# Token-major keys of the mixing stage by a crossbar transpose instead of TensorE, with C and two of the four mixing steps one group later

## Chip, cores, metric

One core of one Trainium2 chip. The metric is the device time of one launch in microseconds (us). Executions of one kernel on a chip mostly agree within 0.3%.

## The reference

Grouped attention (8 batches, 16 query heads, 4 key heads, 384 tokens, head size 64), then a token mixer on its output `x` (8 x 384 x 1024):

```python
wq = x @ w_q                      # d_hyper = 64
wk = x @ w_k
W_tok = einsum('bsd,btd->bst', wq, wk) / 8
mixed = einsum('bst,btd->bsd', W_tok, x)
out = maximum(mixed, 0) @ w_out
```

The kernel reorders the mixing: first `C = wk^T x` (64 x 1024), then `mixed = wq C`. So it needs wk twice turned: the projection makes `qk` with features on the partitions, and C needs wk with tokens on the partitions ("token-major keys").

## The kernel before

Tiles that matter: the projection, the turned keys, C, and the mixing steps (two matmuls each, one relu per matmul on VectorE).

```python
def proj_task(s):                       # 8 matmuls -> pqk, then qk and q2 (VectorE)
    ...
def wk_task(s):                         # token-major keys, TensorE
    ptw = psX.tile([P, C, P], BF16, name="ptw", tag="ps")
    for c in range(C):
        nc.tensor.transpose(out=ptw[:, c, :], in_=s.qk[:, c * P:(c + 1) * P], identity=ident)
    s.wk = m_p.tile([P, C, Dh], BF16, name="wk", tag="wk")
    nc.vector.tensor_copy(out=s.wk, in_=ptw[:, :, Dh:])
def c_task(s):                          # 6 matmuls pc <- wk, xnat; scaled copy to Csb
    ...
def mix_banks(s, i):                    # one mixing step
    for h in range(2):
        pm = psX.tile([P, S], F32, name="pmb", tag="ps")
        nc.tensor.matmul(out=pm, lhsT=s.Csb[r, i*P:(i+1)*P], rhs=..., start=True, stop=True)
        nc.vector.tensor_relu(out=m, in_=pm)
# ... cut ...
elif b < B - 1:                         # batches 2 to 6; g is the batch's first group after it
    at(g + 4, lambda b=b: proj_task(batches[b]), 1.3)
    todo.setdefault(g + 5, []).insert(0, (lambda b=b: wk_task(batches[b]), 0.17))
    todo.setdefault(g + 6, []).insert(0, (lambda b=b: c_task(batches[b]), 0.75))
    gm = (7, 8, 9, 10)                  # groups at whose end a mixing step stands
```

A group is two score tiles (four `sc` matmuls), their exponentials on ScalarE, and then the group's list: AV products (`av`), the tasks above, and single matmuls of the output projection (`po`) as filler. The order is fixed when the program is built. `psX` has four PSUM buffers, shared by everything except the scores. From batch 2 on all input loads, crossbar transposes (`kT`, `qT`, `xT`) and nearly all output writes go through one queue, that of SyncE, in program order.

## Time and profile before

| | before |
|---|---|
| time, median of 4 | 221.97 us (221.65 to 222.37) |
| TensorE, VectorE, ScalarE busy | 94%, 63%, 66% |
| DMA engines | full to 138 us, then 10 to 70% |
| projection of batch 2, 3, 4, 5, 6, 7 starts at | 77.98, 98.92, 122.87, 146.82, 170.55, 188.19 us |

The last row: from one projection to the next is one batch (nine groups; fewer to batch 7), about 24 us for batches 3 to 5 and 20.9 for batch 2. It comes from the timeline of TensorE, the pqk lines.

### The profile page before, as it was taken

How to read it: one execution, taken by the hardware profiler on the slowest of the kernel's cores; microseconds unless marked ns; L12 is line 12 of the kernel's file. 1: busy time of each engine (PE TensorE's matmuls, PEld its weight loads, DVE VectorE, ACT ScalarE, POOL GpSimd, SP SyncE). 2: the span in 40 equal slices, each digit the busy share in tenths (PEclk: the TensorE clock that was granted, in tenths of full speed). 3: DMA queues.
4: the chain of work that ended last, by engine and by line, in shares of the span. 5: the costliest groups of instructions: out<-in, count | busy, mean ns of one | idle time of the engine just before them, and what ended most of it. 6: DMA issues, size and time to landing. Idle time of an engine off the chain costs nothing.

```text
span 220.2 us, 5371 instructions
## 1 busy us (share of the span) xinstructions
PE 208.0 (94%) x2182; PEld 103.9 (47%) x2182; DVE 139.2 (63%) x367; ACT 145.2 (66%) x156; POOL 47.6 (22%) x107
## 2 busy tenths in 40 slices
PE   1899999999999999999999999999999999999991
PEld 0356766554354545454444545445445444443440
DVE  1358868655866466865686568756677579855530
ACT  3799999837799989867767776777777772001100
POOL 1489403525103420350035003400000000000000
PEclk9999999999999999999999999999999999999998
DMA  7999999999959999999999999763531251233243
GB/s 169 308 293 293 234 231 290 202 234 300 219 177 228 270 211 221 236 276 210 296 294 215 226 324 313 210 181 71 172 98 73 98 106 65 95 135 151 98 184 114
DMA packets 75598, 44.71 MB, mean 203 GB/s; under 512 B 45488, under 2 KB 72624, under 8 KB 75568
## 3 DMA queue, kind: packets, MB, share of 16 engines
q1 hardware_dynamic: 72128, 41.69, 75.9%
q0 software_dynamic: 2112, 2.10, 5.6%
q10 hardware_dynamic: 1328, 0.52, 0.9%
q8 instruction: 19, 0.31, 0.6%
q14 instruction: 11, 0.09, 0.1%
HBM read 23.59 MB, written 12.58 MB: 164 GB/s over the span
## 4 chain that ended last, share of the span: by engine, by line
PE 85%; DVE 5%; ACT 5%; DMA 2%; issue 1%
PE po L341 37%; PE sc L189 17%; PE av L207 16%; ACT pT L195 5%; PE pqk L239 4%; PE pmb L317 3%; PE pc L283 2%; DVE xnat L215 2%; DMA qraw<-in_q_dram 2%; PE ptq L176 2%; PE ptx L224 1%; DVE msb L323 1%; PE ptw L274 1%; DVE rcp_all L214 1%; DVE osb L354 1%
## 5 line engine op out<-in xcount | busy, mean ns | idle before, releaser
L195 ACT ACTIVATE pT<-sc 128x1024 bf16<-128x1024 f32 x144 | 139.1, 1026 | 34.4 <-PE sc L189 34.2
L341 PE MATMUL po<-wout_sb,msb 128*128 128x512 bf16 x384 | 101.9, 379 | 0.2 <-DVE osb L354 0.2
L207 PEld LDWEIGHTS <-pT 128*128 128x128 bf16 x1152 | 44.9, 98 | 18.2 <-issue 8.9
L207 PE MATMUL av<-vbf,pT 128*128 128x65 bf16 x1152 | 51.4, 194 | 0.2 <-DVE msb L323 0.2
L189 PE MATMUL sc<-qT,kT 64*128 64x512 bf16 x288 | 49.5, 393 | 1.5 <-DVE qT L131 0.5
L341 PEld LDWEIGHTS <-msb 128*128 128x128 bf16 x384 | 33.1, 97 | 37.1 <-issue 12.3
L215 DVE TENSOR_TENSOR xnat<-av,rcp_all 128x256 bf16<-128x256 f32 x96 | 40.8, 425 | 3.3
L354 DVE COPY osb<-po 128x512 f32<-128x512 f32 x46 | 31.6, 688 | 16.5 <-PE po L341 16.4
L131 POOL CAST qbf<-qraw 128x512 bf16<-128x512 f32 x46 | 26.9, 622 | 25.5 <-DMA qraw<-in_q_dram 22.5
L323 DVE TENSOR_SCALAR msb<-pmb 128x384 bf16<-128x384 f32 x53 | 27.0, 551 | 8.1 <-PE pmb L317 8.1
L214 DVE RECIPROCAL rcp_all<-av 128x4 f32<-128x4 f32 x96 | 17.1, 178 | 19.6 <-PE av L207 19.1
L189 PEld LDWEIGHTS <-kT 64*128 64x128 bf16 x288 | 12.7, 94 | 20.9 <-issue 17.7
L131 POOL CAST kbf<-kraw 128x384 bf16<-128x384 f32 x15 | 7.7, 510 | 66.6 <-DMA kraw<-in_k_dram 66.6
L306 ACT ACTIVATE msb<-pm 128x768 bf16<-128x768 f32 x2 | 1.6, 811 | 19.9 <-PE pm L300 19.9
L239 PE MATMUL pqk<-xT,wqk_sb 128*128 128x384 bf16 x56 | 10.3, 327 | 0.0
L317 PE MATMUL pmb<-qk,Csb 64*128 64x384 bf16 x32 | 9.3, 331 | 0.2 <-DVE Csb L292 0.2
L317 PEld LDWEIGHTS <-Csb 64*128 64x128 bf16 x56 | 3.3, 93 | 11.4 <-issue 6.2
L245 DVE CAST qk<-pqk 128x384 bf16<-128x384 f32 x7 | 3.9, 557 | 7.5 <-PE pqk L239 7.5
L292 DVE TENSOR_SCALAR Csb<-pc 128x512 bf16<-128x512 f32 (+1 forms) x9 | 5.6, 631 | 4.8 <-PE pc L283 4.8
L317 PE MATMUL pmb<-q,Csb 64*128 64x384 bf16 x24 | 8.0, 332 | 0.4 <-DVE xnat L215 0.2
L129 ACT COPY osb<-po 128x256 f32<-128x256 f32 x2 | 0.7, 373 | 11.2 <-DVE osb L131 11.2
L131 POOL CAST vbf<-vraw 128x384 bf16<-128x384 f32 x16 | 8.0, 506 | 0.0
(54 smaller groups left out, 81.3 us busy)
## 6 DMA issues: line engine op xcount, KB each, us to landing
out_dram<-osb SPq DMA_DIRECT2D x23, 512.0 KB, 3.1
qraw<-in_q_dram SPq DMA_DIRECT2D x30, 384.0 KB, 5.0
kraw<-in_k_dram SPq DMA_DIRECT2D x16, 192.0 KB, 4.6
vraw<-in_v_dram SPq DMA_DIRECT2D x16, 192.0 KB, 4.8
wout_sb<-in_moe_w_out_dram POOLq DMA_DIRECT2D x4, 512.0 KB, 12.2
qraw<-in_q_dram SPq DMA_DIRECT2D x1, 512.0 KB, 5.3
qraw<-in_q_dram ACTq DMA_DIRECT2D x1, 256.0 KB, 4.0
wraw<-in_moe_w_q_dram SPq DMA_DIRECT2D x1, 256.0 KB, 6.4
```

Of the source, the lines that this page charges most:

```text
L131: eng.tensor_copy(out=out, in_=in_)
L189: nc.tensor.matmul(out=ps[:, h, :], lhsT=s.kT[r, d, c, :], rhs=s.qT[d][r, j, :, :].rearrange("p g n -> p (g n)"), start=True, stop=True)
L195: nc.scalar.activation(out=s.pT[d, j][:, c, :, :], in_=ps, func=AF.Exp, scale=attn_scale)
L207: nc.tensor.matmul(out=av[:, i, :], lhsT=pT[:, c, h, i * P:(i + 1) * P], rhs=s.vbf[:, g, c, :], start=(c == 0), stop=(c == C - 1))
L214: nc.vector.reciprocal(out=rcp, in_=av[:, :, D])
L215: nc.vector.tensor_tensor(out=s.xnat[:, d, j, h * G * D:(h + 1) * G * D].rearrange("p (i d) -> p i d", i=G), in0=av[:, :, :D], in1=rcp.to_ ...
L239: nc.tensor.matmul(out=s.pqk, lhsT=wqk_sb[:, dc, :], rhs=s.xT[:, dc // (DC // ND), :, dc % (DC // ND), :], start=(dc == 0), stop=(dc == DC ...
L292: eng.tensor_scalar_mul(s.Csb[:, r], pc[:, r], moe_scale)
L317: nc.tensor.matmul(out=pm, lhsT=s.Csb[r, i * P:(i + 1) * P], rhs=(s.qk if h == 0 else s.q2)[r, :], start=True, stop=True)
L323: nc.vector.tensor_relu(out=m, in_=pm)
L341: nc.tensor.matmul(out=po, lhsT=s.msb[:, dc, c * P:(c + 1) * P], rhs=wout_sb[:, dc, half * NH:(half + 1) * NH], start=(n == 0), stop=(n == ...
L354: nc.vector.tensor_copy(out=osb[:, half * NH:(half + 1) * NH], in_=po)
```

## The change

Intent: take three transposes per batch from the bounding engine and a copy from VectorE, use the crossbar instead, and give the transfer a group more before C needs it.

```diff
+    def wk_dma(s):
+        s.wkq = m_p.tile([P, C, P], BF16, name="wkq", tag="wkq")
+        nc.sync.dma_start_transpose(out=s.wkq, in_=s.qk)
+        s.wk = s.wkq[:, :, Dh:]
...
                 at(g + 4, lambda b=b: proj_task(batches[b]), 1.3)
-                todo.setdefault(g + 5, []).insert(0, (lambda b=b: wk_task(batches[b]), 0.17))
-                todo.setdefault(g + 6, []).insert(0, (lambda b=b: c_task(batches[b]), 0.75))
-                gm = (7, 8, 9, 10)
+                at(g + 4, lambda b=b: wk_dma(batches[b]), 0.0)
+                todo.setdefault(g + 7, []).insert(0, (lambda b=b: c_task(batches[b]), 0.75))
+                gm = (8, 9, 9, 10)
```

## The prediction

> **What bounds the kernel now.** I read the page first (busy shares, the 40 slices, the chain), then the chain in order of time, then the timeline and the landing times around the place where batch 2 is mixed, then the order of instructions on TensorE and on the SyncE queue in both kernels.
>
> ```profile
> PE 208.0 (94%) x2182; PEld 103.9 (47%) x2182; DVE 139.2 (63%) x367; ACT 145.2 (66%) x156; POOL 47.6 (22%) x107
> ...
> DMA  7999999999959999999999999763531251233243
> ...
> PE 85%; DVE 5%; ACT 5%; DMA 2%; issue 1%
> ```
>
> TensorE is busy 94% and holds 85% of the chain, so what its stream gains or loses is the time. The second thing to see is the DMA row: full until slice 25 (about 138 us), light after it. Batches are mixed (C, mixing steps) around 82, 104, 128, 152 and 176 us for batches 2 to 6: two or three in the full stretch, two in the light one.
>
> ```profile
> 79.61 0.65 PE L189 MATMUL sc<-qT,kT 64*128 64x512 bf16 x4
> 80.04 1.94 ACT L195 ACTIVATE pT<-sc 128x1024 bf16<-128x1024 f32 x2 [0.22 <-PE sc L189]
> 80.19 0.34 PE L274 MATMUL ptw<-ident,qk 128*128 128x128 bf16 x3
> 80.37 0.54 PE L207 MATMUL av<-vbf,pT 128*128 128x65 bf16 x12
> 80.57 0.26 DVE L277 COPY wk<-ptw 128x192 bf16<-128x192 bf16 x1 [0.23 <-PE ptw L274]
> ...
> 81.65 0.77 PE L189 MATMUL sc<-qT,kT 64*128 64x512 bf16 x4
> ...
> 82.35 0.84 PE L283 MATMUL pc<-xnat,wk 128*64 128x512 bf16 x6
> ...
> 83.03 0.58 SPq L96 DMA_DIRECT2D qraw<-in_q_dram  x1
> 83.66 0.51 SPq L92 DMA_DIRECT2D vraw<-in_v_dram  x1
> 84.27 2.71 SPq L229 DMA_TRANSPOSE xT<-xnat  x1
> ```
>
> This is batch 2 in the timeline. The program runs in groups: two score tiles (four sc matmuls), their two exponentials, then the rest. Three transposes (ptw) occupy the stream from 80.19 to 80.37, and C (pc) starts at 82.35. The SyncE queue is back to back here: it reaches the vraw load only at 83.66.
>
> **What the Trainium skill says.** "VectorE: DVE Perf Modes", section "The three transpose paths", gives 390 ns for a TensorE transpose of 128x128 bf16 and 1309 ns for one by the crossbar. The trace has 219 ns for one ptw, but three cost the stream only 0.18 us because they overlap; so the saving is far smaller than the page's figure suggests. "DMA: Bandwidth & Descriptors", section "Queues, rings and completion order", says that each DMA engine consumes a ring's descriptors in order: a new transfer stands behind those issued before. The trace agrees: vraw of 83.66 lands 4.5 us later, the xT transpose of 84.27 lands 6.7 us later, i.e. at 91.0. "Perfetto Trace Analysis", section "Summary: the profiler window per engine type", says a transfer's bar is only its issue; so landing times must be used, not the 1.3 to 4.2 us bars:
>
> ```profile
> DMA to landing us min/median/max: 3.2/5.2/6.7
> ```
>
> This is the answer for xT: 5 to 6.7 us while the engines are full, 3.2 to 3.7 from 138 us on. "TensorE: Matmul & The Clock Gate", Part 1, says that after about one idle window (3.4 us) the array drops to half rate and needs a busy window to come back. The first microseconds of this trace show such a slow stretch, in the chain:
>
> ```profile
> 12.77 0.54 PE ptq L176 x4
> ...
> 15.40 0.22 PE ptq L176 x4
> ```
>
> **The change part by part.** Removed for batches 2 to 6: 15 TensorE transposes. 0.18 us of stream per three, so 5 x 0.18 = 0.9 us, all on the path: -0.9. Also removed: five VectorE copies of 0.26 us and five PSUM tiles; VectorE is not the bound, so 0 by itself.
>
> Added: five crossbar transposes of three 128x128 blocks on the SyncE queue, and a wait of C for their landing. The order of instructions shows where they stand: behind kT, qT, an output write, qraw and vraw of the same stretch, ahead of the next xT. Moved: C comes one group later, as the first work after that group's scores, and the mixing steps go from one in each of four groups to one, two, one. TensorE takes its stream in order, so if the transpose has not landed, everything waits.
>
> Batch 2: without the transposes the two groups before C are paced by ScalarE (two exponentials of 1026 ns, 2.05 us a group), so the scores of C's new group start near 81.65 + 2.05 = 83.7 and C is due near 84.2. Landing: vraw lands at 83.66 + 4.5 = 88.2. The 12-block xT after it landed 2.8 us later; three blocks are a quarter, 0.7 us, so 88.9. If the moved output write lets the queue run ahead, it could be issued at about 83.2 and land in the light-load 3.2 us, at 86.4. Wait: 2.2 to 4.7 us; I take 4.3, because the engines are full and the bytes ahead are the same. ScalarE has only two exponentials in hand, so it stops too, and nothing makes the time up later: the schedule is fixed and TensorE has the same work left. +4.3.
>
> Batch 3: with the old times the queue would issue it at 104.3 (after the output write of 103.8), landing about 5 us later at 109.3, against C due near 106.8. But the queue keeps draining while TensorE waits in batch 2, and is then held only by xT of batch 3, which needs the delayed tokens. I expect the queue to be about 2 us later than before and TensorE about 4: wait 0 to 1, taken 0.3.
>
> Batches 4 to 6: for batch 4 the queue is free at 126.35, landing 4.1 us later (the landing of the xT of 127.69) is 130.5, C is due after the scores that started at 130.24, about 130.8: 0. For 5 and 6 the cast qk is ready near 149.1 and 172.6, landing in 3.4 us at 152.5 and 176.0; C is due at 155.2 and 178.4: 0.
>
> Mixing steps two to a group: a step is two relus of 551 ns, 1.1 us of VectorE, and that group also has two AV evictions of 0.6 us and a copy of 0.69. In batch 2's stretch VectorE was already busy 3.90 of 4 us (88 to 92). With four PSUM buffers some matmuls will wait for a release: 0.1 us a batch, 0.5 in all, the last batch most (four mixing matmuls back to back after the last scores).
>
> Clock: a hole of 4.3 us contains a whole free-running window of 3.4 us with a chance of (4.3 - 3.4) / 3.4, about 0.3. Then one to two windows at half rate lose 1.7 to 3.4 us, mean 2.5: 0.3 x 2.5 = +0.7. The 3.4 us are the skill's; the trace of before shows no such hole, only the slow start.
>
> Sum: -0.9 + 4.3 + 0.3 + 0 + 0.5 + 0.7 = +4.9, so 222.0 + 4.9 = 226.9 us.
>
> **The rivals.** (1) The wait is hidden: C waits three groups after the projection, 6 to 8 us, more than any landing seen (7.1 at most). Then the time is 222.0 - 0.9 + 0.5 = 221.6. For it: batches 4 to 6 do fit. Against it: what counts is not the time since the projection but since the queue reaches the transpose, and in batch 2 the queue reaches vraw 4 us after the qk cast at 79.5 to 80.1. (2) The hole cools the array: 222.0 - 0.9 + 4.7 + 0.3 + 0.5 + 3 = 229.6. For it, the slow start; against it, the hole is only slightly longer than the window. (3) The wait recurs in batches 2 and 3 in full (no catching up of the queue): -0.9 + 4.7 + 2.5 + 0.5 = +6.8, 228.8. (4) VectorE becomes the bound where two mixing steps meet: five times 0.7 us with no DMA wait, 222.0 - 0.9 + 3.5 = 224.6. Against it: VectorE is at about 70% in the middle of the run.
>
> **Range and chances.** The low end is rival 1 with a short wait of about 1.5 us, 222.6; the high end is rival 2, 230.0. The 2% line is 226.4, just under the estimate, so slower by over 2% gets 0.55 and within 2% gets 0.43. Faster by over 2% would need 4.4 us, five times what is removed: 0.02.
>
> **What would show it.** Right: the transpose of batch 2 issued between 83.2 and 85, landing 4 to 5 us later; TensorE idle 3.5 to 5 us just before the first pc matmul of batch 2, released by that transfer, and ScalarE idle in the same stretch; waits under 1 us before the other four; then every later projection about 4 us later than before. The clock step: four ptw-like or score matmuls at twice their spacing just after the hole. Wrong: no idle time before pc (rival 1), idle time in small pieces released by the relu or by VectorE (rival 4), or a hole at batch 3 as long as at batch 2 (rival 3).

## More of the kernel before

When a group has two mixing steps, the first one stands right after the scores.

The busy share of TensorE hides short waits: a matmul's bar overlaps the next one's, so what counts is the distance between starts.

## The result

The changed kernel takes 227.95 us (median of 4, 227.22 to 229.92), 1.0285 times the time before (95% interval 1.0229 to 1.0342): slower. Ratios are the mean time of one kernel's fast runs over that of the other's in the same rounds, so not quite the ratio of the medians. Executions over 1.5% slower than the fastest of the same kernel are left out of the means. The profiled execution was the slowest of these (229.92), so spans in its trace are up to 2 us longer than the median run's.

The timeline of the changed kernel around C of batch 2 (columns: start us, duration us, engine, line, operation, tile; in brackets the idle time before it and what ended it):

```profile
82.87 1.34 SPq L92 DMA_DIRECT2D vraw<-in_v_dram  x1
...
83.95 0.88 PE L189 MATMUL sc<-qT,kT 64*128 64x512 bf16 x4
...
84.31 1.20 SPq L282 DMA_TRANSPOSE wkq<-qk  x1
...
89.10 1.41 PE L289 MATMUL pc<-xnat,wkq 128*64 128x512 bf16 x6 [4.27 <-DMA wkq<-qk]
90.45 1.46 PE L347 MATMUL po<-wout_sb,msb 128*128 128x512 bf16 x3
...
92.49 1.94 ACT L195 ACTIVATE pT<-sc 128x1024 bf16<-128x1024 f32 x2 [6.17 <-PE sc L189]
```

```profile
DMA to landing us min/median/max: 4.8/4.8/4.8
```

The queue reaches the transpose 4 us after its input is ready (the qk cast ran from 79.80 to 80.36). It lands 4.8 us after its issue (the view of the tile has its time to landing, minimum, median and maximum of this one), TensorE stands still for 4.27 us and ScalarE for 6.17. Then the six pc matmuls take 1.41 us where those of before took 0.84, and three po matmuls 1.46. Dividing the trace of the changed kernel into stretches (columns: stretch, its length, then busy time and instructions of TensorE, weight loads, VectorE, ScalarE, GpSimd, and after them the granted TensorE clock, DMA share, GB/s) shows why:

```profile
84.00:89.00 5.00, 0.73 (x5) 0.15 (x4) 0.44 (x2) 2.32 (x3) 0.00 (x0) 1.00 1.16 253
89.00:92.50 3.50, 3.40 (x13) 0.73 (x13) 0.69 (x1) 0.01 (x1) 1.40 (x3) 0.53 1.05 255
92.50:96.00 3.50, 3.14 (x46) 1.80 (x45) 2.59 (x7) 3.23 (x4) 1.08 (x3) 0.98 0.99 260
```

The stretch after the hole ran at a granted clock of 0.53. So the array was slowed after it had been idle, for about 3.5 us. (In slices of half a microsecond the clock is 0.50 from 89.2 to 92.6 us.)

The rest of the loss is not in the list of waits. Here are the projections of batches 2 and 3, first in the kernel before, then in the changed one:

```profile
77.98 1.47 PE L239 MATMUL pqk<-xT,wqk_sb 128*128 128x384 bf16 x8
...
98.92 1.47 PE L239 MATMUL pqk<-xT,wqk_sb 128*128 128x384 bf16 x8
```

```profile
78.29 1.47 PE L239 MATMUL pqk<-xT,wqk_sb 128*128 128x384 bf16 x8
...
105.72 1.47 PE L239 MATMUL pqk<-xT,wqk_sb 128*128 128x384 bf16 x8
```

The projections of the changed kernel start at 78.29, 105.72, 129.97, 154.22, 178.29 and 196.86 us. Against before that is +0.31, +6.80, +7.10, +7.40, +7.74, +8.67: after the jump in batch 2, each batch loses 0.3 us more and the last 0.9, though three transposes are gone from each. Where this happens, in batch 3 of the changed kernel:

```profile
118.13 0.33 PE L323 MATMUL pmb<-qk,Csb 64*128 64x384 bf16 x1
...
118.29 0.32 PE L323 MATMUL pmb<-q,Csb 64*128 64x384 bf16 x1
...
118.70 1.94 DVE L329 TENSOR_SCALAR msb<-pmb 128x384 bf16<-128x384 f32 x4
118.84 0.33 PE L323 MATMUL pmb<-qk,Csb 64*128 64x384 bf16 x1
...
119.30 0.32 PE L323 MATMUL pmb<-q,Csb 64*128 64x384 bf16 x1
119.76 1.00 PE L207 MATMUL av<-vbf,pT 128*128 128x65 bf16 x24
```

A step's two matmuls use different halves of the array and can start together, as they do at other places (both at 124.1 in this batch). Here the starts are 0.46 us apart, which is near the pace of the relus on VectorE (four in 1.94 us), as if each matmul got a PSUM buffer only when a relu has emptied one. That reading is tested by e3 and e6 below, as far as it is.

### The profile page after: what moved, and what is told of

Read it like the earlier page. It is cut to its first block, busy times and chain, and to the rows that moved or that the text cites.

```text
span 228.1 us, 5350 instructions
## 1 busy us (share of the span) xinstructions
PE 210.6 (92%) x2167; PEld 103.4 (45%) x2167; DVE 137.3 (60%) x362; ACT 145.3 (64%) x156; POOL 47.5 (21%) x107
## 4 chain that ended last, share of the span: by engine, by line
PE 80%; DVE 10%; DMA 4%; ACT 3%; issue 1%
PE po L347 35%; PE sc L189 16%; PE av L207 15%; PE pqk L239 4%; DVE msb L329 4%; DVE xnat L215 3%; PE pc L289 3%; ACT pT L195 3%; DMA wkq<-qk 2%; DMA qraw<-in_q_dram 2%; PE pmb L323 2%; DVE osb L360 2%; PE ptq L176 2%; DVE rcp_all L214 1%; PE ptx L224 1%
## 5 line engine op out<-in xcount | busy, mean ns | idle before, releaser
L207 PEld LDWEIGHTS <-pT 128*128 128x128 bf16 x1152 | 45.5, 98 | 22.5 <-issue 11.3
L207 PE MATMUL av<-vbf,pT 128*128 128x65 bf16 x1152 | 52.0, 194 | 0.7 <-DVE msb L329 0.2
L347 PEld LDWEIGHTS <-msb 128*128 128x128 bf16 x384 | 32.4, 97 | 36.9 <-issue 13.4
L329 DVE TENSOR_SCALAR msb<-pmb 128x384 bf16<-128x384 f32 x53 | 26.5, 549 | 5.3 <-PE pmb L323 5.3
L189 PEld LDWEIGHTS <-kT 64*128 64x128 bf16 x288 | 12.2, 94 | 24.3 <-issue 21.3
L289 PE MATMUL pc<-xnat,wkq 128*64 128x512 bf16 x30 | 4.8, 431 | 4.3 <-DMA wkq<-qk 4.3
```

Source lines behind the costliest of these rows:

```text
L189: nc.tensor.matmul(out=ps[:, h, :], lhsT=s.kT[r, d, c, :], rhs=s.qT[d][r, j, :, :].rearrange("p g n -> p (g n)"), start=True, stop=True)
L207: nc.tensor.matmul(out=av[:, i, :], lhsT=pT[:, c, h, i * P:(i + 1) * P], rhs=s.vbf[:, g, c, :], start=(c == 0), stop=(c == C - 1))
L289: nc.tensor.matmul(out=pc[h * Dh:(h + 1) * Dh, :], lhsT=s.wk[:, c, :], rhs=s.xnat[:, h, c, :], start=(c == 0), stop=(c == C - 1))
L347: nc.tensor.matmul(out=po, lhsT=s.msb[:, dc, c * P:(c + 1) * P], rhs=wout_sb[:, dc, half * NH:(half + 1) * NH], start=(n == 0), stop=(n == ...
```

## Experiments

Twelve runs, in three calls (e1 to e4, e5 to e8, e9 to e12), each call on its own chip; all gave the correct result. Times are medians of all executions, ratios are of the fast ones, against the kernel before in the same rounds. So compare two runs of different calls by their ratios.

| run | what | time us | ratio |
|---|---|---|---|
| e1_batch2_tensor | batch 2 as before | 224.28 | 1.0108 |
| e2_only_batch2 | only batch 2 changed | 224.79 | 1.0137 |
| e3_schedule_only | TensorE transposes, later C and steps | 226.11 | 1.0199 |
| e4_mix_back | changed, steps not paired | 224.79 | 1.0126 |
| e5_late_batches | only batches 4 to 6, steps not paired | 220.48 | 0.9945 |
| e6_tensor_mix_back | TensorE transposes, later C, steps not paired | 221.67 | 1.0009 |
| e7_fill_hole | 18 idle matmuls in the hole | 227.82 | 1.0282 |
| e8_queue_first | transpose of batch 2 ahead of two loads | 226.58 | 1.0226 |
| e9_fill_less | 12 idle matmuls in the hole | 226.68 | 1.0239 |
| e10_changed_again | the changed kernel, beside e9 | 228.22 | 1.0278 |
| e11_idle_transposes | e5 plus transposes nobody reads | 221.00 | 0.9964 |
| e12_batch3_too | e5 plus batch 3 | 222.27 | 0.9987 |

### Which batch, and which part (e1 to e4)

e1 keeps the old branch for batch 2, e2 uses the new one for batch 2 alone:

```diff
+            elif b == 2:   # e1: old branch;  e2: new branch
```

> Batch 2 keeps the TensorE transposes, C and mixing steps of the kernel before; batches 3 to 6 are as in the changed kernel. Theory A (the loss is the wait for the transfer in batch 2 and the slow array after it, about 6 us, plus about 0.3 us a batch where two mixing steps meet): no idle time of TensorE before C anywhere, 222.5 to 223.5 us. Rival B (the later C and the paired mixing steps cost about the same in every batch, 1.2 us each): 226.8 us. Rival C (the wait moves to batch 3, since the SyncE queue no longer gets 4 us to catch up): idle time of 2 to 3 us before C of batch 3, about 225 us.

Measured: 224.28. Too slow for theory A (222.5 to 223.5), well below rival B's 226.8. The waits of TensorE for a transfer (columns: waiting engine and line, releaser, us in total, times, longest) in e1:

```profile
PE pc L289 <- DMA wkq<-qk: 1.4, 1, 1.4
```

It stands before C of batch 3. In the changed kernel batch 3 did not wait; there the queue had caught up during the hole of batch 2. So rival C is partly right: the queue's lag is one debt, paid in batch 2 or, less of it, in batch 3.

> The complement: only batch 2 is changed, batches 3 to 6 are as in the kernel before. Theory A: the same idle time of 4.0 to 4.5 us before C of batch 2 and pc matmuls at half rate after it; 226.5 to 227.5 us. Rival B: 223.2 us. Rival C: as A, 227 us (C differs only in the first run of this group).

Measured: 224.79, two microseconds under theory A and 1.6 above rival B (223.2), with a shorter hole:

```profile
87.17 0.84 PE L289 MATMUL pc<-xnat,wkq 128*64 128x512 bf16 x6 [2.86 <-DMA wkq<-qk]
```

The hole was 2.86 us here and the pc matmuls after it ran at full speed (0.84 us). Batch 2 alone is thus about half of the loss, and batches 3 to 6 hold the other half. Theory A as I had sized it falls.

e3 keeps the transposes on TensorE and only moves C and the steps; e4 is the changed kernel with one line different:

```diff
-                gm = (8, 9, 9, 10)
+                gm = (7, 8, 9, 10)      # e4
```

> TensorE transposes kept in all batches, but C and the mixing steps one group later as in the changed kernel. Theory A: five times about 0.5 us, 223.5 to 224.5 us, with TensorE idle or stretched only where two mixing steps meet. Rival B (the schedule is the whole loss): 227 us or more. Rival D (pairing the mixing steps costs nothing): 222.0 us.

Measured: 226.11 over all four runs; the ratio 1.0199 is from the three fast ones (224.91, 226.73, 225.49), since one of 228.91 counted as slow. Its verdict is "unclear" at 2%, but its interval (1.0153 to 1.0245) is far from no change. This is twice what theory A gave, without a single transfer in the way.

> As the changed kernel, but the mixing steps stay one in each of four groups where they were (C comes at the start of the group whose end has the first step). Theory A: the hole in batch 2 stays 4.0 to 4.5 us; the 0.3 to 0.5 us a batch goes, 225.5 to 226.5 us. Rival D: 228 us. If C's scaling copy is not ready in time for the first step, that shows as TensorE waiting for VectorE before the first mixing matmul, under 0.5 us a batch.

Measured: 224.79, better than expected: undoing the pairing gives back about 3 us of the 6. The hole of batch 2 stays (3.92 us), with a slow array after it (clock 0.56 in the 3.5 us that follow). From projection to projection e4 needs 23.55 us in batches 3 and 4, where the kernel before needs 23.95.

### Later C or paired steps (e6)

> TensorE transposes in all batches, C one group later, mixing steps where they were: against the third run it takes away only the pairing of mixing steps, against the fourth only the crossbar. If the pairing is what cost 0.5 us and more a batch: 221.5 to 222.3 us, each batch about 23.7 us from projection to projection. If the later C itself costs: 224 us or more, as in the third run.

Measured: 221.67, ratio 1.0009 (0.9984 to 1.0033). C one group later costs nothing that these runs can show. e3 and e6 differ in one line, `gm`: it pairs two mixing steps, and it also moves the first two steps one group later. That line is e3's whole loss: 1.9% of the time before, about 4 us by the timed runs and 3.2 us by the traces (batches 2 to 6 took 21.80, 24.41, 24.42, 24.47, 18.52 us in e3 and 21.13, 23.95, 23.94, 23.74, 17.63 in e6, from projection to projection). No run moved the steps later without pairing them (8, 9, 10, 11), so that the pairing and not the later place costs the time is read from the timelines. Two groups of batch 3 in both, e3 first (its second group has one mixing step more, its first has as many):

```profile
109.09 0.60 PE L189 MATMUL sc<-qT,kT 64*128 64x512 bf16 x4
...
111.56 0.33 PE L323 MATMUL pmb<-qk,Csb 64*128 64x384 bf16 x1
...
111.72 0.32 PE L323 MATMUL pmb<-q,Csb 64*128 64x384 bf16 x1
...
111.82 0.65 PE L189 MATMUL sc<-qT,kT 64*128 64x512 bf16 x4
...
112.13 1.94 DVE L329 TENSOR_SCALAR msb<-pmb 128x384 bf16<-128x384 f32 x4
112.27 0.33 PE L323 MATMUL pmb<-qk,Csb 64*128 64x384 bf16 x1
112.73 0.32 PE L323 MATMUL pmb<-q,Csb 64*128 64x384 bf16 x1
113.19 1.00 PE L207 MATMUL av<-vbf,pT 128*128 128x65 bf16 x24
...
115.17 0.59 PE L189 MATMUL sc<-qT,kT 64*128 64x512 bf16 x4
```

and e6:

```profile
109.18 0.59 PE L189 MATMUL sc<-qT,kT 64*128 64x512 bf16 x4
...
112.11 0.67 PE L189 MATMUL sc<-qT,kT 64*128 64x512 bf16 x4
112.47 1.01 DVE L329 TENSOR_SCALAR msb<-pmb 128x384 bf16<-128x384 f32 x2
112.71 0.55 PE L207 MATMUL av<-vbf,pT 128*128 128x65 bf16 x12
...
114.83 0.59 PE L189 MATMUL sc<-qT,kT 64*128 64x512 bf16 x4
```

From scores to scores the second group takes 3.35 us in e3 and 2.72 us in e6; part of this is the step that e3 has more there. The first takes 2.73 and 2.93. The whole batch, with the same work in it, is 0.46 us longer in e3. In e3 the last step of the group before meets the first step of the pair: four relus stand in a row on VectorE, and nothing that needs a PSUM buffer goes on faster than they do. That the buffers are the link is read from the starts; no run had more buffers in `psX`, so it is not shown by experiment.

### The place in the queue (e8)

```diff
                 at(g + 4, lambda b=b: wk_dma(batches[b]), 0.0)
+                if b == 2:   # these two loads stood one group earlier
+                    at(g + 4, lambda: batches[5].parts[1](), 0.0)
```

> The changed kernel with two loads (384 and 192 KB) moved from just before the transpose of batch 2 to just after it on the SyncE queue; nothing else. If the wait is set by the place in the queue: the transpose is issued at about 82.4 instead of 84.3 us and lands about 2 us earlier, the wait before C falls from 4.3 to 2 to 2.5 us, the array stays at full rate, and the time falls by 3 to 4 us to 224 to 225 us. Rival (the transfer lands when the DMA engines have room, whatever its place): wait and time as in the changed kernel.

Measured: 226.58, outside the expected 224 to 225, but the wait of batch 2 did fall:

```profile
86.72 0.84 PE L289 MATMUL pc<-xnat,wkq 128*64 128x512 bf16 x6 [1.75 <-DMA wkq<-qk]
```

The transpose was issued at 83.27 and landed 3.4 us later, where in the changed kernel it took 4.8 from 84.31. In that trace TensorE waits 3.1 us for wkq in two places: 1.36 us of it stands before C of batch 3, as in e1. This is one trace, and the issue alone would not show it: it came 4.8 us after the start of the projection, and with the old order 4.8 (e9) to 6.2 us (e10). The landing does: 8.3 us after that start, where the old order gave 9.5 (e2, e9) to 10.8 us (changed kernel). So the place in the queue shortens the wait, but the next batch pays part of the debt.

### The slow array (e7, e9, e10)

```diff
+    def keep_warm():                       # before C of batch 2; the result is not read
+        pd = psX.tile([P, NH], F32, name="pd", tag="ps")
+        for n in range(18):                # 12 in e9
+            nc.tensor.matmul(out=pd, lhsT=ident, rhs=wout_sb[:, n % DC, :NH], ...)
```

> The changed kernel with 18 matmuls of 512 columns, whose result nobody reads, just before C of batch 2 (3.9 us at full rate, so they fit into the wait of 4.3 us). If the slow array after the hole is real and comes from its idleness: C of batch 2 at the same time as before, its matmuls 380 ns and not 632, and 1.5 to 2 us less than the changed kernel: about 226 us. Rival (the slowness after the hole comes from elsewhere, a backlog of VectorE or of the transfers): no gain, 228 us, or more by what the extra matmuls overrun.

Measured: 227.82, no gain: the first half of the expectation held (pc matmuls in 0.84 us) and the time did not. In this trace the transfer had landed at 87.65 (83.25 + 4.4) and C could start only at 88.59, after the extra matmuls: they overran by 0.9 us. That makes the run inconclusive for the time, so it was repeated with fewer matmuls beside the changed kernel.

> As the seventh run with 12 matmuls instead of 18 (2.6 us), so that they no longer overrun the landing; about 1.5 us of the wait stays idle. If the slow array costs 1 to 2 us: no pc matmul over 400 ns, 1 to 2 us less than the changed kernel in the same rounds, 226 to 227 us. Rival (what looks slow after the hole costs nothing in the end, since ScalarE and VectorE set the pace there): same time as the changed kernel.

> The changed kernel once more, beside the ninth run on the same chip: 227.5 to 228.5 us, the wait before C of batch 2 4 to 4.6 us, its first pc matmuls at about 630 ns.

Measured: 226.68 against 228.22 in the same rounds; by the ratios 1.0239 against 1.0278, 0.9 us, by the medians 1.5. The intervals (1.0208 to 1.0270 and 1.0245 to 1.0311) overlap, so the size is loose. The traces give a larger price. From the start of C of batch 2 to the projection of batch 3, with the same TensorE tasks, it is 16.62 us in the changed kernel and 17.53 in e10, but 14.81 and 14.82 in e9 and e7 (15.19 and 15.02 in e2 and e8, whose shorter holes slowed nothing): 1.4 to 1.8 us for the slow array of the changed kernel, 2.3 to 2.7 for that of e10. Not every execution pays it: the mean clock of ten of the eleven timed executions of the changed kernel is 0.982 to 0.993, that of the fastest (226.56) is 1.0 (the kernel before: 0.993 to 1.0). The clock itself is not in doubt. e9, the stretch from C on:

```profile
87.00:92.50 5.50, 5.22 (x65) 2.50 (x65) 3.60 (x9) 3.56 (x4) 2.19 (x4) 1.00 1.23 200
```

and e10, whose hole was 3.88 us:

```profile
84.10:87.80 3.70, 0.00 (x0) 0.00 (x0) 0.00 (x0) 1.38 (x2) 0.00 (x0) 0.89 1.18 256
87.80:91.30 3.50, 3.43 (x13) 0.78 (x13) 0.69 (x1) 0.00 (x0) 1.47 (x3) 0.50 1.12 259
91.30:95.00 3.70, 3.64 (x36) 1.85 (x34) 1.95 (x6) 2.36 (x3) 1.29 (x4) 0.66 0.91 239
```

Holes of 4.27, 3.92 and 3.88 us (the changed kernel, e4, e10) were followed by a clock of 0.50 to 0.56; holes of 2.86 and 1.75 us (e2, e8) by full clock. This agrees with the 3.4 us that the Trainium skill gives in "TensorE: Matmul & The Clock Gate", Part 1, but not in every detail: in slices of half a microsecond e10's clock falls at 87.0, only 3.0 us after its last matmul ended (83.99, an end that the profile models). It stays at 0.50 until 93.8, 6.8 us, where the changed kernel and e4 have 3.4; that is why e10 pays more.

### What the transposes are worth (e5, e11, e12)

e5 uses the old branch for batches 2 and 3, where the queue is late, and for 4 to 6 the crossbar without pairing.

> Batches 2 and 3 as in the kernel before; batches 4 to 6 by the crossbar transpose, C one group later, but the mixing steps one in each of four groups as before. Read from the fourth run, where such a batch took 23.55 us against 23.95 before: three times 0.4 us gained and no wait for the transfer, 220.3 to 220.8 us, 0.5% faster. Rival: the gain was that chip's or that execution's, and only the 0.18 us of stream per batch is real: 221.2 us, not to be told from before.

Measured: 220.48, ratio 0.9945 (0.9931 to 0.9960): faster than both kernels, though by less than 2%, with no wait for a transfer.

```diff
+    def idle_transposes(s):     # e11 = e5 and these, in batches 4 to 6; C still reads wkq
+        ptw = psX.tile([P, C, P], BF16, name="ptw", tag="ps")
+        for c in range(C): nc.tensor.transpose(out=ptw[:, c, :], in_=s.qk[:, c*P:(c+1)*P], ...)
```

> As the fifth run, but the three TensorE transposes of batches 4 to 6 are done as well (C still reads the crossbar's result; the VectorE copy is not made). If the gain is the 0.18 us of stream per three transposes, it goes by 0.54 us: 221.0 us. If the larger part is the removed VectorE copy and its wait, little goes: 220.5 to 220.7 us.

Measured: 221.00, ratio 0.9964 (0.9951 to 0.9976). Against e5, from projection to projection, batches 4 to 6 took 23.93, 23.58, 17.72 us instead of 23.76, 23.41, 17.56: 0.17, 0.17 and 0.16 us for three transposes each, which is the 0.18 of the prediction. By the timed runs e11 is still 0.36% faster than before, about 0.8 us. Hardly any of that stands in the three batches: against before they gain 0.59 us in e5 and 0.09 in e11. The stretch after the last projection is shorter, 31.2 and 31.3 us instead of 32.0. So the removed copy of 0.26 us and its wait are worth little in these traces; why the end is shorter (the filler matmuls are spread differently) no run tells.

> As the fifth run, with batch 3 by the crossbar too, and two loads moved behind its transpose on the SyncE queue as in the eighth run. In the first run batch 3 waited 1.4 us; the place gained is worth about 1.2 us and C is due later by the pairing that is gone. Wait 0 to 0.5 us, time 220.1 to 220.6 us, not to be told from the fifth run; without the effect of the place, 221.5 us.

Measured: 222.27 over 22 runs; the ratio 0.9987 (0.9968 to 1.0006) is from the 15 fast ones. The time missed the expected 220.1 to 220.6. As expected batch 3 no longer waits for the transfer, but in the profiled execution batch 4 then did, 0.77 us. Seven runs counted as slow (223.74 to 225.09); they were not profiled and are not explained. So in that trace the lag of the queue reaches batch 4, and e5 is the better version.

## Why the prediction was right

It said 226.9, and 227.95 was measured. Its mechanism holds: a transfer late in the queue, one hole in batch 2, none later. Two of its terms were too small, and that the total still came so near is partly luck.

- **Transposes removed, -0.9.** Right in what it counts: 0.17 us per batch by e11, five times that is 0.85. The timed runs give e5 1.04 us for three batches, twice as much, but in the traces most of the rest stands after the last projection (see e11); the prediction has no term for it.
- **Wait in batch 2, +4.3.** Right, to the place and the size: issue at 84.31, landing 4.8 us later, 4.27 us of idle time before pc. In other executions of the same branch it was 2.9 to 3.9.
- **Batch 3, +0.3, and batches 4 to 6, 0.** Right: no wait in the changed kernel. The reason given, that the queue drains during the hole, is supported by e1, where there is no hole and batch 3 waits 1.4 us.
- **Slow array, +0.7.** It came, and in each of the three traces with a hole over 3.4 us, so the chance of 0.3 was too low, and rival 2, which was set aside, describes the profiled execution. It lasted one or two times 3.4 us, as the prediction said for the case that it comes. Its price is 0.9 to 1.5 us by the timed runs of e9 and e10, 1.4 to 2.7 by the traces.
- **Two mixing steps in a group, +0.5 in all.** This step failed in size: "0.1 us a batch, 0.5 in all". It measures 3.2 us (traces) to 4 us (runs). That is rival 4's figure, 0.7 us a batch, which was set aside because "VectorE is at about 70% in the middle of the run". The average says nothing about four relus in a row in front of four PSUM buffers.
- **The sum.** It can be checked in the profiled executions. From the projection of batch 2 to that of batch 7 the measured sizes give -0.85 + 4.3 + 1.4 to 1.8 + 3.2 = 8.0 to 8.4 us, an estimate; measured 8.67 - 0.31 = 8.36. The 0.3 us that each later batch loses is the pairing (0.46 and 0.48 us in batches 3 and 4) less the transposes (0.17). After the last projection 0.8 us come back (31.2 us against 32.0), so the spans differ by 7.9 us, 228.1 against 220.2. The timed medians differ by 6.0 only, since the profiled execution was the slowest; how long the hole and the slow array were in the others is not recorded. So 2.7 us missing in the pairing and about 1 in the slow array were made up by a shorter end and by executions that lost less than the profiled one.

"Every later projection about 4 us later" was too low, 6.8 to 8.7 us: the slow array and the pairing come on top of the hole. Among the working's small figures, the low end of the range (222.6) does not follow from rival 1 with a wait of 1.5 us: 221.6 + 1.5 is 223.1.

## What to carry to other kernels

When work moves from a full engine to a transfer, count from the moment at which the in-order queue reaches the transfer, not from the moment at which its input is ready; here that is 4 us in the stretch with full DMA engines and next to nothing later, so the same change loses in batch 2 and gains in batches 4 to 6. Move the consumer later without crowding what follows it: two evictions more in one group cost more than the transposes that were saved. And judge such crowding from the distance between starts around the buffers, not from busy shares.

## What the Trainium skill lacked or had wrong

- "VectorE: DVE Perf Modes", section "The three transpose paths", prices a TensorE transpose at 390 ns; as three in a row within a full stream they cost 0.17 us together (e11 against e5), about 0.06 us each, so the figure is not what a transpose takes from a full stream.
- The same table gives 1309 ns for a crossbar transpose of one block and does not say what the time covers. Here three blocks needed 2.4 to 5.5 us from issue to landing (five transposes in e10), and up to 4 us more before the queue reached them. No page that I used prices that time before the issue.
- "TensorE: Matmul & The Clock Gate", Part 1, was right about the idle window in size: holes of 3.88 to 4.27 us were followed by a clock of 0.50 to 0.56, those of 2.86 and less were not. But where it asks for at least one idle window of about 3.4 us, e10's clock fell 3.0 us after the modelled end of the last matmul.
- No page that I used says that a matmul's wait, here read as one for a PSUM buffer, can vanish in its bar: in e3, 3.2 us were lost while TensorE showed 94% busy and no single wait over 0.3 us for VectorE at the mixing matmuls. The weight loads before these show a little more (2.8 us for xnat in eight waits, against 1.9 in six in e6).
